# Pairing the 64-token ends of two sequences into one 128-row block, with a new order of all tasks and no filler matmuls, in a sliding-window attention and squared-ReLU kernel

## The chip, the cores and the metric

The kernel runs on one core of a Trainium2 chip, as one launch. Its time is the device time of that core in microseconds (us); the figure quoted for a kernel is the median of its runs. The engines are named as in the profile: PE is TensorE (matrix products; PEld its weight loads), DVE is VectorE, ACT is ScalarE, POOL is GpSimd, SP is SyncE. POOL here does nothing but start transfers that convert f32 to bf16 on the way in; SP starts the transposing transfers and the stores.

## The reference

The computation is attention with a causal window of 128 tokens and a linear distance bias, then a two-layer block with a squared ReLU:

```python
# q, k, v: (8 batches, 8 heads, 576 tokens, 64); w_in: (512, 2048); w_out: (2048, 512); f32
scores = scale * np.matmul(q, k.transpose(0, 1, 3, 2))
rel = pos[:, None] - pos[None, :]
mask = (rel >= 0) & (rel < 128)
scores = np.where(mask, scores + bias[None], -1000000000.0)   # bias = slope of the head * -|rel|
attn = softmax(scores)
x = np.matmul(attn, v)            # reordered to (4608 tokens, 512)
g = np.maximum(x @ w_in, 0.0) ** 2
out = g @ w_out                   # (4608, 512)
```

## The kernel before, in words

**Blocks and jobs.** A sequence of 576 tokens is cut into four blocks of 128 tokens and a last one of 64; the 40 blocks of the 8 sequences are numbered `m` = 0 to 39 in the order of the list `seq`. Blocks 0 to 3 are the first blocks of four sequences ("lone" jobs, with an additive bias). Every other block attends to itself and to the block before it. A "full" job does one 128-token block; a "half" job does the 64-token ends of two sequences together: blocks 10 and 11, 18 and 19, 28 and 29, 38 and 39. The names of tasks carry the block: `lkq10` and `lv10` load keys, queries and values (POOL; for the first blocks `lk`, `lq`, `lv`), `kqT10` transposes keys and queries by a transposing transfer (SP; for blocks 0 to 7 it is `tp`, four PE transposes each for keys and queries, with evictions `ev`), `s10.0` and `s10.1` are the scores (PE), `e10.0` to `e10.3` the exponentials (ACT), `m10.0` and `m10.1` the products with the mask (DVE), `pv10.0` and `pv10.1` the products with the values (PE), `r` and `n` the reciprocal and the normalisation (DVE), `x10` the transpose of the result into `xT` (SP; for blocks 0 to 7 `xp` on PE and an eviction).

**Half jobs before.** The two ends of a half job share the four score banks, but each is a block of its own in every other step: its own load, its own 64-row transpose `kqT`, its own 16 + 16 value products with 64 stationary columns, its own reciprocals and normalisations over 64 partitions, its own 64-row `x`. Because a 64-token block fills half of its tile, the other half of three tiles is set to zero once (`zero...` tasks).

**The two layers.** Tokens are taken in 9 groups `g` of 512. For groups 0 to 2 the first layer runs in units (`u0.1.2` is group 0, row range 1, step 2): in group 0, range 0 (the first block) steps 0 and 1 use `w_in0` and `w_in1` (two of 16 column chunks each), and steps 2, 3, 4 use `w_in2`, `w_in3`, `w_in4` (four each); in ranges 1 to 3 step 0 uses `w_in0` and `w_in1`, step 1 `w_in2`, step 2 `w_in3`, step 3 `w_in4`. From group 3 on the first layer is done by Strassen products `f3.0.1` to `f3.3.7`; the second layer is done by Strassen products `p0.1.0` to `p8.7.1` for all groups. Sums of the operands (`S`, `ut`, `us`, `ws`) are on DVE; snapshots `s1`, `s2`, `s5` and sums `c11`, `c12`, `c22` of products on ACT and DVE; squares `sq` on either; stores `st` on SP.

**Order.** Nothing is ordered by a loop. A string `ORDER` lists all 1722 tasks with the engine that does each (no letter: PE; `a` ACT, `d` DVE, `g` POOL, `s` SP) and, after it, the PSUM bank or ring buffer that it takes. Each engine carries its own tasks out strictly in the order of the string, each when its inputs, its buffers and its turn are there. `transpose_kq` makes every transposing transfer `kqT` wait for all pieces of both weight matrices. The ring of key and query tiles has four places, that of transposed ones seven, that of value tiles nine. The queue of POOL's transfers, and that of SP's, have eight semaphores each.

**Warm-up and fillers.** `warm_up` issues `N_WARM` matmuls of 512 columns on a zeroed tile before anything is there to compute. `fill` adds 128-column matmuls ahead of a task of the first 30 us where the planner expects PE to wait over 400 ns, for the part `FILL` of that wait. Both compute nothing that is used.

Of the kernel before, what the change touches and what calls it, by code (L numbers as in the profile page):

```python
# [27 lines left out]
N_WARM = 8  # L28
# [4 lines left out]
FILL = 0.4  # L33
# [15 lines left out]
NF = 8  # L49
UT = 1  # L50
# [12 lines left out]
iota:g ident:d dist1:d slope1.0:d warm0:d lk0.1:a lk0.0:s one0.1:d slope0.3:d slope1.2:a slope0.0:a one0.3:d  # L63
slope1.1:d slope0.1:a slope1.3:a ck0:a slope0.2:a warm::0 b0::1,2 lk2:g lq2:g lq0.0:s lq0.1:s lk1:g cq0:a
one0.0:d tp0.0::3 tp2.0::4 b2::5,6 tp0.1::7 tp2.1::0 ev2.0.0:d ev0.1.0:a lk3:g lq1:g tp3.0::4 ev3.0.0:a
ev2.1.0:d ev0.0.0:d one0.2:d tp1.0::7 s2 s0 e0.0:a e2.0:a e2.1:a ev1.0.0:d e0.1:a lv0:g lv2:g lq3:g lv1:g
w_in1:g w_in0:g w_in2:g lv3:g w_in3:g lk4:g lq4:g b1::0,4 tp1.1::3 pv2.0::7 ev1.1.0:d r2.0:d pv0.0::1 pv0.1::5
s1 n2.0:d r0.1:d r0.0:d n0.0:d tp3.1::3 n0.1:d xp0.0::6 pv2.1::2 x0.0:d r2.1:d ev3.1.0:d mask1.1:a e1.0:a e1.1:a
table:a pv1.0::7 pv1.1::1 b3::5,0 n2.1:d u0.0.1::4 r1.0:d r1.1:d n1.0:d n1.1:d xp2.0::6 s3 u0.0.0::3 xp1.0::2
dist0:d x2.0:a e3.0:a x1.0:a mask1.7:a reluu0.0.0:a:0 u0.2.0::7 mask0.3:a mask1.2:a mask0.1:a mask1.6:a e3.1:a  # L70
u0.1.0::1 u0.1.1::6 pv3.0::5 pv3.1::2 u0.2.1::3 u0.0.2::0 squ0.0.0:d one1.2:d reluu0.1.0:a:1 mask0.2:a
reluu0.2.0:a:2 one1.8:d r3.0:d squ0.1.0:d one1.7:d r3.1:d n3.0:d n3.1:d xp3.0::1 x3.0:d one1.5:d reluu0.2.1:a:3
one1.6:d squ0.2.1:d squ0.2.0:d reluu0.1.1:a:0 mask1.5:a mask1.4:a mask0.7:a mask0.5:a mask1.3:a mask1.0:a
reluu0.0.2:a:1 u0.1.2::7 tp4.0::5 tp4.1::2 ev4.1.0:d squ0.0.2:d u0.2.2::3 ev4.0.0:a reluu0.0.1:a:3 s4.0::6,1
s4.1::0,5 reluu0.1.2:a:2 e4.0:a lk5:g reluu0.2.2:a:1 lk6:g lq5:g lv5:g lq6:g w_in4:g tp5.0::2 u0.0.3::4
u0.3.0::7 tp5.1::6 squ0.0.1:d one1.1:d one1.0:d squ0.1.2:d ev5.0.0:d e4.1:a mask0.0:a mask0.4:a mask0.6:a m4.0:d
ev5.1.0:d squ0.1.1:d lk7:g lv4:g lv6:g lq7:g w_out3:g w_out0:g lv7:g w_out2:g w_out1:g e4.3:a reluu0.3.0:a:3
e4.2:a reluu0.0.3:a:2 squ0.3.0:d u0.3.1::2 tp6.0::3 reluu0.3.1:a:0 ev6.0.0:d tp6.1::1 s5.0::5,7 ev6.1.0:d
one1.4:d one1.3:d squ0.0.3:d s5.1::6,0 u0.3.2::4 e5.0:a s6.0::3,2 s6.1::1,5 e5.1:a e5.3:a e6.0:a e5.2:a
squ0.2.2:d m4.1:d squ0.3.1:d m5.0:d u0.1.3::7 u0.2.3::0 pv4.0::3 m5.1:d r4.0:d n4.0:d e6.2:a e6.1:a  # L80
reluu0.3.2:a:3 e6.3:a pv4.1::6 pv5.0::1 pv5.1::2 tp7.0::4 u0.0.4::3 tp7.1::5 reluu0.2.3:a:2 ev7.0.0:a
reluu0.0.4:a:1 ev7.1.0:a r5.0:d r4.1:d r5.1:d m6.0:d n5.0:d n5.1:d n4.1:d u0.3.3::0 m6.1:d xp5.0::4 xp4.0::1
pv6.0::2 reluu0.3.3:a:0 x4.0:a squ0.0.4:d x5.0:d squ0.2.3:d pv6.1::3 r6.0:d squ0.3.2:d us0.0:d us3.0:d
squ0.3.3:d S1.0.0:d s7.0::6,5 reluu0.1.3:a:1 s7.1::0,4 u1.0.3::1 e7.0:a e7.2:a e7.1:a e7.3:a u1.0.6::7 u1.0.2::6
u1.0.1::0 reluu1.0.6:a:2 squ1.0.6:a u1.0.4::5 m7.0:d n6.0:d u1.0.7::4 S2.0.0:d m7.1:d lkq9:g lkq8:g lkq10:g
lv9:g lkq11:g kqT9:s r6.1:d us1.0:d n6.1:d xp6.0::7 reluu1.0.1:a:3 reluu1.0.7:a:0 squ1.0.1:a reluu1.0.2:a:2
pv7.1::2 pv7.0::0 r7.0:d r7.1:d n7.0:d u1.0.0::3 squ0.1.3:d n7.1:d zerokqT10:d S1.0.1:d S2.0.1:d us2.0:d ws0.0:d
S3.0.0:d u1.0.5::4 xp7.0::0 p0.2.0::6 p0.1.0::2 p0.1.1 ws0.1:d kqT8:s lv8:g reluu1.0.4:a:3 x6.0:a squ1.0.2:a
x7.0:a reluu1.0.3:a:1 squ1.0.3:d u1.1.1::5 reluu1.1.1:a:2 reluu1.0.0:a:1 squ1.0.0:a squ1.0.4:d squ1.0.7:d
zerov10:d s1_0:d:0 kqT10:s ws1.0:d zerokqT11:d kqT11:s squ1.1.1:d p0.2.1 u1.1.5::7 u1.1.0::0 reluu1.1.0:a:3  # L90
reluu1.0.5:a:0 reluu1.1.5:a:1 u1.1.7::1 squ1.1.0:d ws1.2:d reluu1.1.7:a:2 u1.1.2::5 u1.1.6::3 squ1.1.7:a
reluu1.1.2:a:3 reluu1.1.6:a:2 u1.1.3::0 lkq12:g lv12:g lkq13:g lkq14:g s8.0::4,7 s8.1::1,5 ws0.2:d c11_0:d
S4.0.1:d S4.0.0:d squ1.1.5:d e8.0:a e8.1:a e8.2:a e8.3:a p0.5.0::6 u1.1.4::3 s9.0::4,7 s9.1::1,5 p0.5.1 kqT12:s
m8.0:d ws1.1:d m8.1:d reluu1.1.4:a:1 e9.0:a e9.1:a pv8.1::3 pv8.0::4 p0.6.0 p0.6.1 squ1.1.4:d S1.1.0:d
reluu1.1.3:a:1 e9.2:a s5_0:a:1 e9.3:a p0.3.0 lv10:g lv13:g lkq15:g m9.0:d r8.0:d n8.0:d squ1.0.5:d pv9.0::7
zerov11:d m9.1:d r8.1:d us0.1:d S3.0.1:d pv9.1::0 p0.3.1 lv11:g r9.1:d n8.1:d s10.0::1,4 s10.1::5,3 ws1.3:d
squ1.1.6:a s2_0:a:2 c12_0:d us3.1:d r9.0:d n9.0:d n9.1:d ws0.3:d e10.0:a e10.2:a e10.3:a m10.1:d us2.1:d e10.1:a
squ1.1.2:a x8:s p0.7.0 p1.2.0::6 p1.2.1 s12.0::1,5 s12.1::7,3 p0.7.1 lkq16:g e12.0:a e12.3:a squ1.1.3:a e12.2:a
e12.1:a x9:s m10.0:d S2.1.0:d us1.1:d pv10.0::0 pv10.1::4 pv11.0::1 c22_0:d r11.0:d p1.1.0::3 p1.1.1 p0.4.0
# [146 lines left out]
class Plan:  # L246
# [27 lines left out]
    def order(self):  # L274
# [8 lines left out]
        for item in ORDER.split():  # L283
            if item.startswith("reluc"):
                continue
# [51 lines left out]
def kernel(  # L337
# [196 lines left out]
    def zero(m, tag, slot, key, part, after):  # L534
        def run():
            if slot.turn == 0:
                nc.vector.memset(part(tile_of(slot)), 0.0)
# [917 lines left out]
```

## Time and profile before

| | |
|---|---|
| median of 3 runs | 292.15 us (291.11, 292.15, 292.66) |
| profiled execution, its own time | 291.41 us |
| its span, first to last instruction | 289.6 us |
| PE busy | 281.0 us, 3480 matmuls |
| DVE, ACT, POOL busy | 242.5, 202.3, 106.3 us |
| read from and written to memory | 36.70 MB and 9.44 MB |

The profiled execution took 1.8 us more than its span, which is what lies around the instructions; its time is 0.74 us under the median of the runs. A busy share says how much of the span an engine had an instruction under way. Matmuls overlap: one takes some 270 ns from start to end while the next starts after 109 ns, so PE's mean durations are latencies, and what a stream of them costs is read from the starts of neighbouring rows.

### The profile page before, as it was taken

How to read it: one execution, taken by the hardware profiler on the slowest of the kernel's cores; microseconds unless marked ns; L12 is line 12 of the kernel's file. 1: busy time of each engine (PE TensorE's matmuls, PEld its weight loads, DVE VectorE, ACT ScalarE, POOL GpSimd, SP SyncE). 2: the span in 40 equal slices, each digit the busy share in tenths (PEclk: the TensorE clock that was granted, in tenths of full speed). 3: DMA queues.
4: the chain of work that ended last, by engine and by line, in shares of the span. 5: the costliest groups of instructions: out<-in, count | busy, mean ns of one | idle time of the engine just before them, and what ended most of it. 6: DMA issues, size and time to landing. Idle time of an engine off the chain costs nothing.

```text
span 289.6 us, 8647 instructions
## 1 busy us (share of the span) xinstructions
PE 281.0 (97%) x3480; PEld 243.5 (84%) x3480; DVE 242.5 (84%) x570; ACT 202.3 (70%) x399; POOL 106.3 (37%) x132
## 2 busy tenths in 40 slices
PE   6999999999999999999999999999999999999994
PEld 2688999887888988888888889888898888888884
DVE  2555897799858899999899999999998988998764
ACT  4669985877388785799888978797774834845700
POOL 8967734492662940542738363060000000000000
PEclk9999999999999999999999999999999999999999
DMA  9999999999999999999999999999421122010054
GB/s 127 166 194 171 183 201 160 140 135 155 184 153 177 174 151 181 176 160 189 168 166 180 176 184 153 162 114 175 129 75 57 54 69 63 20 36 2 0 162 148
DMA packets 171495, 39.62 MB, mean 137 GB/s; under 512 B 156992, under 2 KB 171456, under 8 KB 171456
## 3 DMA queue, kind: packets, MB, share of 16 engines
q0 software_dynamic: 115184, 18.10, 88.8%
q1 hardware_dynamic: 55520, 20.39, 39.2%
q10 hardware_dynamic: 752, 0.59, 0.7%
q8 instruction: 27, 0.44, 0.6%
q14 instruction: 12, 0.10, 0.1%
HBM read 36.70 MB, written 9.44 MB: 159 GB/s over the span
## 4 chain that ended last, share of the span: by engine, by line
PE 77%; DMA 8%; POOL 7%; ACT 2%; DVE 2%; issue 1%; POOLq 0%
PE o L1246 32%; PE h L1091 25%; PE h L997 10%; PE pv L848 5%; PE s L738 5%; DMA kq<-in_q_dram 4%; DMA vt<-in_v_dram 2%; DMA kqT<-kq 2%; POOL kq L612 2%; POOL kq L618 2%; POOL vf L625 1%; POOL w_in_sb L549 1%; ACT g L956 1%; DVE P L760 1%; ACT rt L964 1%
## 5 line engine op out<-in xcount | busy, mean ns | idle before, releaser
L1246 PEld LDWEIGHTS <-g 128*128 128x128 bf16 x704 | 67.8, 98 | 8.0
L772 ACT ACTIVATE P<-s 128x512 bf16<-128x512 f32 x120 | 65.0, 620 | 6.9 <-PE s L738 6.6
L964 ACT ACTIVATE rt<-h 128x512 bf16<-128x512 f32 (+1 forms) x73 | 42.4, 602 | 22.2 <-PE h L997 11.4
L618 POOL DMA_DIRECT2D kq<-in_k_dram x32 | 27.2, 851 | 76.6 <-DMA kqT<-kq 72.6
L1246 PE MATMUL o<-w_out_sb,g 128*128 128x256 bf16 x432 | 54.0, 273 | 0.0
L1112 DVE CUSTOM_DVE_ANT_0 rt<-h,f 128x512 bf16<-128x512 f32 x72 | 48.5, 683 | 6.1 <-PE h L1091 2.8
L450 ACT ACTIVATE f<-h 128x512 f32<-128x512 f32 x63 | 36.5, 604 | 19.0 <-PE h L1091 17.5
L956 ACT ACTIVATE g<-rt 128x512 bf16<-128x512 bf16 x70 | 42.9, 636 | 6.2 <-DVE rt L1112 5.8
L997 PE MATMUL h<-xT,w_in_sb 128*128 128x128 bf16 (+1 forms) x512 | 46.6, 246 | 0.5 <-DMA w_in_sb<-in_moe_w_in_dram 0.5
L997 PEld LDWEIGHTS <-w_in_sb 128*128 128x128 bf16 x512 | 39.1, 98 | 4.7 <-DMA w_in_sb<-in_moe_w_in_dram 0.9
L1091 PE MATMUL h<-xT,w_in_sb 128*128 128x256 bf16 x288 | 41.7, 273 | 0.0
L1091 PEld LDWEIGHTS <-w_in_sb 128*128 128x128 bf16 x384 | 36.0, 98 | 5.0
L760 DVE TENSOR_TENSOR P<-P,masks 128x1024 bf16<-128x1024 bf16 x48 | 32.3, 683 | 4.1 <-ACT P L772 3.3
L1246 PE MATMUL o<-wsum,sums 128*128 128x256 bf16 x288 | 35.7, 273 | 0.0
L1246 PE MATMUL o<-wsum,g 128*128 128x256 bf16 x272 | 34.8, 273 | 0.0
L958 DVE TENSOR_TENSOR g<-rt 128x512 bf16<-128x512 bf16 (+1 forms) x75 | 29.8, 413 | 4.8 <-ACT rt L964 4.7
L625 POOL DMA_DIRECT2D vt<-in_v_dram x36 | 30.8, 871 | 4.4 <-DMA w_in_sb<-in_moe_w_in_dram 2.1
L877 DVE TENSOR_TENSOR x<-pv,rec 128x256 bf16<-128x256 f32 (+1 forms) x80 | 31.6, 414 | 0.7
L1091 PEld LDWEIGHTS <-us 128*128 128x128 bf16 x288 | 27.8, 98 | 3.5
L1246 PEld LDWEIGHTS <-sums 128*128 128x128 bf16 x288 | 27.6, 98 | 3.6
L450 ACT ACTIVATE f<-o 128x512 f32<-128x512 f32 x30 | 18.2, 608 | 14.6 <-PE o L1246 13.3
L618 POOL DMA_DIRECT2D kq<-in_q_dram x32 | 27.5, 860 | 2.0 <-PE xp L897 1.8
(79 smaller groups left out, 356.9 us busy)
## 6 DMA issues: line engine op xcount, KB each, us to landing
out_dram<-f SPq DMA_DIRECT2D x62, 128.0 KB, 2.5
kq<-in_k_dram POOLq DMA_DIRECT2D x31, 128.0 KB, 6.1
kq<-in_q_dram POOLq DMA_DIRECT2D x31, 128.0 KB, 7.0
vt<-in_v_dram POOLq DMA_DIRECT2D x28, 128.0 KB, 6.4
w_out_sb<-in_moe_w_out_dram POOLq DMA_DIRECT2D x4, 512.0 KB, 11.5
w_in_sb<-in_moe_w_in_dram POOLq DMA_DIRECT2D x3, 512.0 KB, 8.7
out_dram<-f SPq DMA_DIRECT2D x13, 64.0 KB, 2.2
vf<-in_v_dram POOLq DMA_DIRECT2D x4, 128.0 KB, 4.7
```

The lines of the kernel that those rows point to most:

```text
L450: nc.scalar.activation(o, i, AF.Copy)
L618: nc.gpsimd.dma_start(view(kq[s_kq[m].idx], i), source(src, m, split))
L625: nc.gpsimd.dma_start(tile_of(s_v[m])[0:n, :, 0:D], source(v, m))
L760: nc.vector.tensor_tensor(flat(Pt[sP.idx], w), flat(Pt[sP.idx], w), flat(masks, w), op=ALU.mult)
L772: nc.scalar.activation(flat(Pt[sP.idx], slice(2 * i, 2 * i + 2)), sS[i].tile.rearrange("p (j t) -> p j t", j=2)[:, :, lo:hi], AF.Exp, bias ...
L877: nc.vector.tensor_tensor(o, heads(sv)[0:n, :, 0:D], sr.tile[0:n, :].unsqueeze(2).to_broadcast([n, 4, D]), op=ALU.mult)
L956: nc.scalar.activation(o, i, AF.Square, bias=0.0, scale=1.0)
L964: nc.scalar.activation(rts[srt.idx][:, 0:n], slot.tile[:, 0:n], AF.Relu, bias=0.0, scale=1.0)
L997: nc.tensor.matmul(slot.tile[:, f * w:(f + 1) * w], w_in_sb[:, cc, fc * 128:(fc + 1) * 128], xT[:, cc, lo % (XR * 128):lo % (XR * 128) + w ...
L1091: nc.tensor.matmul(slot.tile[:, j * 256:j * 256 + 256], a, b_, start=fresh and j == 0 and c == 0, stop=c == 1, skip_group_check=True)
L1112: nc.vector._custom_dve(TENSOR_ADD_SAT, out=rts[srt.idx], in0=slot.tile, in1=other(), s0=FMAX, s1=0.0)
L1246: nc.tensor.matmul(slot.tile[:, z * 256:z * 256 + 256], stationary(c), moving(c), start=fresh and z == 0 and c == 0, stop=c == F - 1, skip ...
```

## The change

1. **Ends paired.** The ends of two sequences become one block of 128 rows under the number of the first (10, 18, 28, 38): they are loaded into the two halves of one tile (six transfers as before, of 64 rows each), transposed by one `kqT`, normalised by two `r` and two `n`, and transposed by one `x`. The tasks of blocks 11, 19, 29 and 39 and the `zero` tasks are gone. A new mask `pmask` (`pm0`, `pm1`, `pm2`) is built once in the place of two tiles of the first blocks, after the scores that read these tiles.
2. **Value products of a pair.** Eight products with 128 stationary columns against the pair's own values, then sixteen with 64 stationary columns, alternately for the first and the second sequence, whose results go to partitions 0 to 63 and 64 to 127.
3. **A new `ORDER`** of 1677 tasks, on each engine and in all banks; 43 tasks move from DVE to ACT, 38 from ACT to DVE, two stores from SP to ACT.
4. **`FILL` 0.4 to 0.0, `N_WARM` 8 to 12.**
5. **Dependencies.** Products `f.1` and `f.2` wait for the first half of their group's tokens only; tiles of values, of the first blocks' keys and of `ut` are given free by each reader; the second part of `S1` and `S2` comes after the first.

```diff
-N_WARM = 8
+N_WARM = 12
-FILL = 0.4
+FILL = 0.0
...
+    pmask = kqf[:, 0:2].rearrange("p l c t -> p (l c t)").rearrange("p (h r t) -> p h r t", h=H, r=2)
...
+    def load_pair(m, key):
...
+                for j in range(2):
+                    o = kq[s_kq[m].idx][64 * j:64 * j + 64, i * d_model:(i + 1) * d_model]
+                    nc.gpsimd.dma_start(o.rearrange("s (h d) -> s h d", h=H), source(src, m + j))
...
-            pieces = [(part * 128 + i * 64, 64, part, (before[m], m)[part], m)
-                      for part in range(2) for i, m in enumerate(ms)]
+            pieces = [(i * 64, 64, before[m], ms[0], i * 64) for i, m in enumerate(ms)] + [(128, 128, ms[0], ms[0], 0)]
...
+        def pv_pair():
...
+            for h in range(H):
+                sv, hi = svs[h // 4], h % 4
+                nc.tensor.matmul(sv.tile[:, hi * (D + 1):(hi + 1) * (D + 1)], Pt[sP.idx][:, place(h), 1],
+                                 tile_of(s_v[m])[:, h, 0:D + 1], start=hi == 0, stop=False, skip_group_check=True)
+            for h in range(H):
+                sv, hi = svs[h // 4], h % 4
+                for i2, mk in enumerate(mb):
+                    nc.tensor.matmul(sv.tile[64 * i2:64 * i2 + 64, hi * (D + 1):(hi + 1) * (D + 1)],
+                                     Pt[sP.idx][:, place(h), 0, 64 * i2:64 * i2 + 64],
+                                     tile_of(s_v[mk])[:, h, 0:D + 1], start=False, stop=True, skip_group_check=True)
...
-        rel = [s_t] if u == 3 and p in (4, 5, 6) else []
-        tm = plan.add({"PE": 4 * mm(256)}, key, emit, deps + st["x"],
+        rel = [s_t] if p in (4, 5, 6) else []
+        tm = plan.add({"PE": 4 * mm(256)}, key, emit, deps + st["xe" if p < 3 else "x"],
```

The head of the order, PE's tasks alone, before and after:

```
before: warm b0 tp0.0 tp2.0 b2 tp0.1 tp2.1 tp3.0 tp1.0 s2 s0 b1 tp1.1 pv2.0 pv0.0 pv0.1 s1 tp3.1 xp0.0 pv2.1 pv1.0
        pv1.1 b3 u0.0.1 xp2.0 s3 u0.0.0 xp1.0 u0.2.0 u0.1.0 u0.1.1 pv3.0 pv3.1 u0.2.1 u0.0.2 xp3.0 u0.1.2 tp4.0 tp4.1 ...
after:  warm tp0.0 tp3.0 tp0.1 b3 b0 tp1.0 s0 tp3.1 s3 tp1.1 tp2.0 b1 tp2.1 pv0.1 pv3.0 s1 pv3.1 b2 pv1.0 pv0.0 xp3.0
        pv1.1 tp4.0 s2 xp0.0 xp1.0 u0.0.2 pv2.0 u0.1.1 tp4.1 pv2.1 u0.3.1 u0.0.1 s4.0 s4.1 xp2.0 u0.1.0 u0.2.1 u0.3.0
        u0.2.0 u0.3.2 u0.0.0 tp5.0 tp7.0 tp5.1 ...
```

And of POOL:

```
before: iota lk2 lq2 lk1 lk3 lq1 lv0 lv2 lq3 lv1 w_in1 w_in0 w_in2 lv3 w_in3 lk4 lq4 lk5 lk6 lq5 lv5 lq6 w_in4 lk7 lv4
        lv6 lq7 w_out3 w_out0 lv7 w_out2 w_out1 lkq9 ...
after:  iota lk2 lk3 lk1 lq3 lq2 lq1 lv0 lv3 lv1 lk4 w_in2 lv2 lq4 w_in1 w_in0 lk5 w_in3 lk7 lq5 lq7 lv4 w_in4 lv5 lv7
        lk6 lq6 w_out0 w_out1 lv6 lkq10 lkq8 w_out3 lkq9 w_out2 lv9 ...
```

More of the change, by code (lines that the diff above doesn't have):

```diff
@@ L62 @@
 ORDER = """
[L63 to L67, printed above, removed]
@@ L83 @@
[L83 to L87, printed above, removed]
@@ L530 @@
                                  name=f"one1.{i}", later=20000.0)
[L534 to L537, printed above, removed]
-        return plan.add({"DVE": 220.0}, key, run, [], [slot], name=f"zero{tag}{m}", later=25000.0, after=after)
     t_win = [None] * FCB
@@ L702, in job @@
         nb = len(ms)
-        n = 64 if kind == "half" else 128
-        for m in ms:
+        for m in ms[:1] if kind == "half" else ms:
             transpose_kq(m, due)
@@ L1055, in prepare_up @@
         xs = [x for m in blocks(g * 512, g * 512 + 512) for x in t_x[m]]
+        xe = [x for m in blocks(g * 512, g * 512 + 256) for x in t_x[m]]
         ts = []
```

260 lines of the change are left out of this document (72 added, 188 removed).

## The prediction

> **What bounds the kernel now.** I read the page first (busy times, slices, chain), then PE's waits, then PE's timeline.
>
> ```profile
> span 289.6 us, 8647 instructions
> PE 281.0 (97%) x3480; PEld 243.5 (84%) x3480; DVE 242.5 (84%) x570; ACT 202.3 (70%) x399; POOL 106.3 (37%) x132
> ...
> PE   6999999999999999999999999999999999999994
> ...
> PEclk9999999999999999999999999999999999999999
> DMA  9999999999999999999999999999421122010054
> ...
> PE 77%; DMA 8%; POOL 7%; ACT 2%; DVE 2%; issue 1%; POOLq 0%
> ```
>
> PE never leaves nine tenths after the first slice: the time is PE's head, the sum of PE's work, the few holes, and the tail. The transfers are as full as PE until 215 us. PE's waits, in total (engine, line, releaser: us, times, longest):
>
> ```profile
> PE wm L649 <- DVE sums L468: 2.5, 1, 2.5
> PE pv L848 <- DMA vt<-in_v_dram: 0.5, 1, 0.5
> PE pv L848 <- ACT P L813: 0.5, 2, 0.3
> PE h L997 <- DMA w_in_sb<-in_moe_w_in_dram: 0.5, 1, 0.5
> PE tp L681 <- DMA kq<-in_q_dram: 0.5, 1, 0.5
> ```
>
> Only 4.5 us are waits. Four stand before 25 us; the other, 0.5 us at 70 us, is for the values of block 11. So there is little to win in the middle. From PE's timeline (start, us, what, count) and the chain of waits, the rows for the prices:
>
> ```profile
> 2.50 3.59 PE L649 MATMUL wm<-sums 128*128 128x512 bf16 x8 [2.50 <-DVE sums L468]
> 5.88 1.06 PE L796 MATMUL s<-sums,ident 128*128 128x512 bf16 x2
> ...
> 19.51 1.07 PE L997 MATMUL h<-xT,w_in_sb 128*128 128x128 bf16 x16 [0.47 <-DMA w_in_sb<-in_moe_w_in_dram]
> ...
> 24.61 0.40 PE L681 MATMUL tp<-ident,kq 128*128 128x128 bf16 x4 [0.45 <-DMA kq<-in_q_dram]
> ...
> 51.06 5.40 PE L997 MATMUL h<-xT,w_in_sb 128*128 128x256 bf16 x48
> 56.39 0.23 PE L738 MATMUL s<-kqT,kqT 64*128 64x128 bf16 x2
> ...
> 56.94 1.05 PE L1246 MATMUL o<-wsum,sums 128*128 128x256 bf16 x8
> ...
> 112.65 1.04 PE L1246 MATMUL o<-wsum,sums 128*128 128x256 bf16 x8
> 113.62 1.20 PE L848 MATMUL pv<-vt,P 128*64 128x65 bf16 x32
> 114.75 0.61 PE L1091 MATMUL h<-xT,w_in_sb 128*128 128x256 bf16 x4
> ```
>
> ```profile
> 13.98 10.58 DMA kq<-in_q_dram
> 26.79 1.79 PE h L997 x32
> ...
> 47.51 6.37 DMA kqT<-kq
> ...
> 64.15 6.68 DMA vt<-in_v_dram
> ...
> 271.74 12.23 PE o L1246 x112
> 283.97 1.78 PE o L1348 x24
> ```
>
> Prices: 12.23 / 112 = 109 ns for 256 columns, 1.79 / 32 = 56 ns for 128. Scores: the 48 matmuls before them end their issue at 51.06 + 48 x 0.109 = 56.30, the scores start at 56.39 and give way at 56.94; their eight pairs of row halves stream 8 x 0.056 = 0.45. So a run of scores costs 0.19 us beyond its work, 0.09 to go in and 0.10 to go out. A run of 64-column value products costs the same: 113.62 - (112.65 + 8 x 0.109) = 0.10 to go in, then 1.13 for 32, of which 32 x 0.0315 = 1.01 stream and 0.1 goes out.
>
> **The head.** I measure PE by its lag: the start of a task less the useful PE work ahead of it in the order, at these prices (value products 30 ns, a pair of 512-column bias matmuls 0.43 us). Ahead of the first scores of block 8 stand 256 unit matmuls of 128 columns (14.3 us), 15 units of group 1 and 4 products of 8 x 0.109 (16.6), 24 groups of four transposes (5.4), biases and lone scores (3.3), four score jobs (2.5) and the value products (2.8): 44.9 us. They start at 56.39, lag 11.5. At `tp4.1`, the row at 24.61, 13.3 us stand ahead: lag 11.3. There the lag was made, by queries 4, which landed at 13.98 + 10.58 = 24.56; afterwards PE loses almost nothing. So the new lag decides, and the new lag is set by when weights land.
>
> ```profile
> w_in_sb<-in_moe_w_in_dram POOLq DMA_DIRECT2D x3, 512.0 KB, 8.7
> ...
> kq<-in_q_dram POOLq DMA_DIRECT2D x31, 128.0 KB, 7.0
> ```
>
> ```profile
> 5.00:10.00 5.00, 4.86 (x39) 2.91 (x37) 1.39 (x4) 1.77 (x3) 5.00 (x6) 1.00 2.33 157
> 34.00:37.00 3.00, 3.00 (x72) 3.00 (x70) 2.58 (x11) 2.98 (x7) 2.21 (x3) 1.00 1.25 206
> 30.00:40.00 10.00, 10.00 (x207) 9.34 (x205) 9.18 (x29) 9.95 (x21) 5.33 (x7) 1.00 1.69 188
> ```
>
> The last column is GB/s: 128 KB of keys at 157 take 0.84 us, 512 KB of weights at 206 take 2.5. Queries 4 were the 12th block after 12 chunks of weights (1.25 us for two). In the new order of POOL `w_in2` has 10 blocks ahead and is chunks 1 to 4: 24.56 - 2 x 0.84 - 8 x 0.63 = 17.8. `w_in0` has 12 blocks and completes 8 chunks: 24.56 - 2.5 = 22.0. `w_in3` has 13 blocks and 12 chunks: 25.4. The PE work ahead of their first users is 6.75 us (`u0.0.2`), 11.2 (`u0.1.0`) and 14.75 (`u0.3.2`): lags 11.1, 10.8, 10.6. The new head is bound by `w_in2`, lag 11.1: it gains 0.4 us. Other bound: should the early `w_in2` come sooner than the later anchor says, `w_in3`, one block behind that anchor, still holds the lag at 10.6, a gain of 0.9. On the other side ACT could be the limit:
>
> ```profile
> L495 ACT ACTIVATE masks<-sums 128x128 bf16<-128x128 f32 x16 | 3.9, 311 | 0.0
> ```
>
> 18 evictions at 9.95 / 21 = 0.47 and 13 masks at 3.9 / 16 = 0.24 make 11.6 us between the start of `u0.0.2` and the end of `u0.2.2`, whose PE work is 10.9: 0.7 more lag, a loss of 0.3. I take the gain of 0.4, because most of those masks can wait for a later eviction.
>
> **Warm-up and fillers: zero.** The fillers are these:
>
> ```profile
> L429 PE MATMUL pv<-sums 128*128 128x128 bf16 x9 | 0.8, 219 | 0.0
> L429 PE MATMUL xp<-sums 128*128 128x128 bf16 x7 | 0.6, 219 | 0.0
> ```
>
> 16 x 0.056 = 0.9 us, all ahead of value products and transposes that then waited for data before 15 us. `warm` stands behind two small memsets in the new order of DVE instead of mask preparation, so it can start near 1.4 instead of 2.50; 12 x 0.42 ends near 6.5 (before: 5.88). PE then has 6.75 us of work for the 11.4 us until `w_in2`, so 4.6 us cover it. Without that cover four more warm matmuls cost 4 x 0.42 = 1.7.
>
> **The pairs.** Before, the ends' value products are 32 matmuls per job in seven runs of the order (blocks 10/11 two, 18/19 one, 28/29 one, 38/39 three). After: 8 of 128 columns and 16 of 64 per job, four runs. Removed 4 x 8 x 0.030 = 0.96 and 3 x 0.19 = 0.57. The scores of a pair stay (16 row-half pairs of 64 against 8 of 64 and 4 of 128), but the new order has 35 runs of scores for 33: +0.38. Sum: -1.15 us of PE work, all on the path. Unknown is a 64-column matmul whose neighbour uses the other column half: as dear as now (0.0315), as cheap as the row halves, which go two in 56 ns, so half the price (another 4 x 16 x 0.016 = 1.0 off), or a change of mode each time (below). I take the first, the nearest row. By the Trainium skill, TensorEngine Tiling (Array Packing), Key Properties, a change of the mode drains the engine but different tiles load and multiply in parallel; the 0.10 at each end agrees, and with the parallel halves the sum would be 1.0 us better. No run so far shows column halves in turn.
>
> DVE loses half of these (off the path, DVE being 84% busy):
>
> ```profile
> L864 DVE RECIPROCAL rec<-pv 64x4 f32<-64x4 f32 x16 | 2.5, 166 | 1.3 <-PE pv L848 1.2
> L877 DVE TENSOR_TENSOR x<-pv,rec 64x256 bf16<-64x256 f32 x16 | 6.4, 408 | 0.2
> ```
>
> 4.4 us less; the mask copies `pm0`, `pm1` go to ACT (about 1 us each, 70% busy) long before block 10's mask. POOL issues as many transfers; SP eight transposes fewer:
>
> ```profile
> L666 SPq DMA_TRANSPOSE kqT<-kq x32: 1193/1414/4038, 47.5 to 196.5; - x32
> ...
> DMA to landing us min/median/max: 2.6/6.1/10.9
> ```
>
> That frees 8 x 1.4 = 11 us of SP, which nobody waits for.
>
> **The holes.** The wait of 0.5 at 70 us goes: values 10 and 11 are one load, ahead of `lv13`, and `pv10` has 63.1 us of work ahead, 74.2 with the lag, against 64.15 + 6.68 = 70.8 for the old landing of the last end. What is late next: the shortest distance between a product and the one that must wait for its snapshot is 0.87 us of PE work in the new order (five places) for 0.91 in the old, where PE waited nowhere; 0.04 short five times, +0.2. The looser dependencies (part 5) remove waits that the trace doesn't have: zero.
>
> **Sum.** -0.4 - 1.15 - 0.5 + 0.2 = -1.9 us: 287.7 span, 289.5 for the profiled execution. That lies 0.7 under the median, so for the median 292.15 - 1.9 = 290.2. For scale, about 0.5%, 1.5 us, is what a measurement here can tell from no change: this lies just beyond. With the bounds above (-0.9 - 2.15 - 0.5 = -3.55; +0.3 - 1.15 - 0.5 + 0.5 = -0.85) the likeliest case runs from 288.6 to 291.3.
>
> **Rivals.**
>
> *The order gives back what the pairs win (no difference).* ACT is late in the new head (+0.3 instead of -0.4), and five snapshots and one load stall 0.2 more each (+1.2): 290.2 + 0.7 + 1.2 = 292.1. For it: the whole order is new, and ACT has 11.6 us of work for 10.9 of PE's. Against: distances that matter have grown (median from scores to value products 5.7 us to 10.0 of PE work). Chance 0.20.
>
> *Transposes come late (slower).* All `kqT` wait for all weights. Before, `kqT9` went at 47.51, when queries 9, two blocks behind the last weight, had landed: the weight landed at 45.8. `w_out2`, now the last weight, stands behind `lkq10` (four half blocks), `lkq8` and `lkq9` (four blocks) besides: 45.8 + 4 x 0.42 + 4 x 0.84 = 50.9. `kqT8` is third on SP, issued at 50.9 + 2 x 1.4 = 53.7; the scores of block 8 have 48.5 us of work ahead, 59.6 with the lag, and block 8's exponentials, masks and value products queue behind them. A latency up to 5.9 costs nothing, the median 6.1 costs 0.2; from 5.9 + 1.9 + 1.5 = 9.3 on it makes the kernel slower by over 1.5 us, and the longest, 10.9, costs 5.0: 295.2. For it: the 6.37 of the first transpose lay on the chain. Against: that one was the first of its burst, and the third is issued 2.8 us later, into fewer loads. Chance 0.12.
>
> *Column halves change mode (slower).* 16 matmuls x 4 jobs x 0.10 = 6.4: 296.6. Only a change of tile size shows 0.10; a change of row half shows none. Chance 0.06.
>
> *The clock falls without fillers.* PE has nothing to do for 4.6 us in all before 17.8, spread by loads that arrive one by one; the first matmuls show a slow clock, (5.88 - 2.50) / 8 = 0.42 us for 512 columns where 256 later take 0.109. A fall would cost half of a stretch like that of these rows, (5.88 - 2.50) / 2 = 1.7 us: 291.9, no measurable difference. By the Trainium skill, TensorE: Matmul & The Clock Gate, Part 1 (The HAM clock gate), an idle window of about 3.4 us halves the clock; no gap in this trace is long enough to show it, the longest wait after the start being 0.5. Between arrivals some work always falls due, so I expect under 3 us in one piece. Chance 0.06.
>
> **How the numbers follow.** Likeliest case 0.56, of which 0.51 over 1.5 us faster (up to 290.7) and 0.05 between that and 291.3; return 0.20 and clock 0.06 end level; late transposes 0.12 and mode changes 0.06 end slower. So faster 0.51, same 0.05 + 0.20 + 0.06 = 0.31, slower 0.18. The range takes in the likeliest case, a little lower for prices rounded up, and the two that end level, to 293.3; it leaves out what is slower.
>
> **What would show it.** Right: 3480 - 16 - 64 + 4 = 3404 matmuls and the first unit at 17.5 to 18.2; block 8's scores at 59 to 60 without a wait; a pair's value products in 0.9 us; PE's waits after 20 us under 1 us; last matmul near 283.7. Wrong: PE waiting on kqT near 60 us, matmuls of 0.1 us in the pairs, 107 ns units near 18 us, or PE idle before ACT's results between 18 and 31 us.

## The result: 304.3 us, 3.6% slower than before

The changed kernel took 304.29 us (median of four runs; 301.16 to 306.15), the kernel before, run beside it, 292.40. The ratio of their runs is 1.036, with a 95% interval of 1.024 to 1.048. The prediction, 290.2 with a range up to 293.3, was wrong in sign. Ratios, here and below, leave out runs over 1.5% above the fastest of the same kernel, which the medians still contain; where a median and a ratio seem to disagree (e12, e17), that is why.

The profiled execution took 304.97 us. Its page:

```profile
span 302.8 us, 8461 instructions
PE 282.4 (93%) x3403; PEld 242.2 (80%) x3404; DVE 241.8 (80%) x557; ACT 203.9 (67%) x397; POOL 106.3 (35%) x132
...
PE   7889999899589999899899976999999999999995
...
PEclk9999999999899999999999998999999999999999
...
PE 54%; DMA 30%; POOL 8%; SPq 3%; issue 3%; ACT 1%; DVE 0%; POOLq 0%; ACTq 0%; DVEq 0%
```

PE, under nine tenths before in the first and the last slice alone, now falls below it in seven slices between 50 and 200 us; the granted clock falls in two of them; and transfers hold 30% of the chain that ended last, where they held 8%. Who waited (in total, times, longest):

```profile
POOL kq L480 <- DMA kqT<-kq: 59.4, 11, 11.7
...
ACT f L294 <- DMA out_dram<-f: 8.3, 4, 2.8
...
PE pv L715 <- DMA vt<-in_v_dram: 3.8, 1, 3.8
...
DVE f L292 <- DMA out_dram<-f: 2.7, 1, 2.7
PE s L609 <- DMA kqT<-kq: 2.5, 2, 1.2
PE o L1135 <- DVE f L292: 2.4, 1, 2.4
...
PE h L980 <- ACT f L294: 2.3, 3, 1.3
...
PE h L885 <- DMA xT<-x: 1.0, 1, 1.0
```

POOL's long wait for transposes is not new. Before, it was longer:

```profile
POOL kq L618 <- DMA kqT<-kq: 72.6, 15, 11.0
```

Two families of new waits are to be seen. In the first, PE waits for what transfers bring: values of pair 10, transposed keys, transposed rows. In the second, PE waits for a snapshot (`f`) that ACT or DVE could not write, because the buffer was still being stored. Before, ACT and DVE never waited for a store to write a snapshot; here they do for 11 us, of which 1.2 stand at 292 us, in the tail. The chain of waits shows one of each (start, us, what):

```profile
45.15 8.42 DMA kq<-in_q_dram
53.57 6.92 DMA kqT<-kq
...
66.21 9.60 DMA kq<-in_q_dram
...
79.68 8.41 DMA xT<-x
...
88.23 1.91 PE h L885 x16
...
180.34 5.44 DMA out_dram<-f
185.86 0.70 DVE f L292
186.60 1.87 PE o L1135 x8
```

From 45 to 88 us no step of the chain is computation: a load lands at 53.6, its transpose at 60.5; that frees the place for the next loads, of which one lands at 75.8; SP issues the transpose of that one and only then, in its strict order, the store and the rows `xT` that PE takes at 88.2. At 186 us a store lands, the snapshot takes its buffer, and PE goes on.

The clock, by stretches (length, PE busy and matmuls, ..., granted clock in the third column from the end):

```profile
79.00:80.00 1.00, 0.81 (x25) 0.75 (x26) 0.12 (x1) 0.00 (x0) 0.66 (x2) 1.00 1.59 158
80.00:81.00 1.00, 1.00 (x9) 0.86 (x9) 1.00 (x5) 0.00 (x0) 0.22 (x1) 0.83 1.92 167
83.00:84.00 1.00, 1.00 (x24) 0.91 (x18) 0.00 (x0) 0.96 (x2) 1.00 (x2) 0.50 2.22 153
84.00:85.00 1.00, 1.00 (x13) 0.80 (x9) 0.00 (x0) 0.78 (x2) 0.34 (x1) 0.96 1.88 208
```

The wait of 3.8 us ends at 79.2; from 80.7 to 84.1 the clock is half. It is half again from 186.5 to 189.9, around the end of the wait of 2.4. The mean granted clock of the execution is 0.988, so 302.8 x 0.012 = 3.6 us of matmul time are lost, 3.4 of them in these two falls of 3.41 us each (the rest lies at the very end).

**Where the time lies.** For each pair of neighbouring matmuls I take the time between their starts less the price of the first (0.215 us for 512 columns, 0.109 for 256, 0.056 for 128, 0.029 for 65, half of that for scores in row halves) and add up, from the first matmul on, which starts at 2.5 us before and at 1.3 after. By this sum PE's work is 266.1 us before and 264.9 after; what is lost beyond it (us, profiled executions):

| lost in | before | after | e6 | e14 | e16 | e5 | e15 |
|---|---|---|---|---|---|---|---|
| 0 to 50 us | 7.7 | 8.5 | 8.6 | 8.7 | 8.9 | 7.0 | 8.5 |
| 50 to 100 | 3.4 | 9.6 | 10.3 | 6.9 | 3.5 | 3.5 | 2.3 |
| 100 to 200 | 4.3 | 12.9 | 6.1 | 5.0 | 4.7 | 4.5 | 5.0 |
| later | 1.6 | 1.6 | 1.3 | 1.1 | 1.0 | 0.7 | 0.8 |

The work fell by 1.2 us, close to the 1.15 forecast; the loss behind 50 us rose by 14.8. The rest of this document is about that rise.

### The profile page after: what moved, and what is told of

The parts are those of the page before. It is cut to its first block, busy times and chain, and to the rows that moved or that the text cites. A ratio compares the mean times of both kernels' runs of the same rounds, so it can differ in the third digit from the quotient of the medians.

```text
span 302.8 us, 8461 instructions
## 1 busy us (share of the span) xinstructions
PE 282.4 (93%) x3403; PEld 242.2 (80%) x3404; DVE 241.8 (80%) x557; ACT 203.9 (67%) x397; POOL 106.3 (35%) x132
## 4 chain that ended last, share of the span: by engine, by line
PE 54%; DMA 30%; POOL 8%; SPq 3%; issue 3%; ACT 1%; DVE 0%; POOLq 0%; ACTq 0%; DVEq 0%
PE o L1135 24%; PE h L980 19%; DMA out_dram<-f 8%; DMA kq<-in_q_dram 8%; PE h L885 5%; DMA kqT<-kq 4%; DMA w_out_sb<-in_moe_w_out_dram 4%; DMA w_in_sb<-in_moe_w_in_dram 3%; PE s L609 3%; DMA xT<-x 3%; POOL kq L474 3%; PE pv L738 2%; SPq L540 2%; POOL kq L480 2%; ACT f L294 1%
## 5 line engine op out<-in xcount | busy, mean ns | idle before, releaser
L641 ACT ACTIVATE P<-s 128x512 bf16<-128x512 f32 x120 | 65.9, 610 | 12.9 <-PE s L609 12.8
L1001 DVE CUSTOM_DVE_ANT_0 rt<-h,f 128x512 bf16<-128x512 f32 x72 | 48.2, 685 | 10.6 <-PE h L980 6.5
L294 ACT ACTIVATE f<-h 128x512 f32<-128x512 f32 x61 | 35.5, 601 | 23.4 <-PE h L980 10.7
L480 POOL DMA_DIRECT2D kq<-in_k_dram x24 | 21.5, 895 | 60.5 <-DMA kqT<-kq 59.4
L980 PE MATMUL h<-xT,w_in_sb 128*128 128x256 bf16 x288 | 40.1, 273 | 0.5 <-ACT f L294 0.4
L1135 PE MATMUL o<-wsum,sums 128*128 128x256 bf16 x288 | 37.7, 281 | 2.9 <-DVE f L292 2.4
L1135 PEld LDWEIGHTS <-sums 128*128 128x128 bf16 x288 | 28.4, 100 | 7.3 <-issue 3.5
L765 DVE TENSOR_TENSOR x<-pv,rec 128x256 bf16<-128x256 f32 x72 | 29.1, 419 | 1.0
L485 POOL DMA_DIRECT2D vt<-in_v_dram x28 | 25.4, 923 | 4.7 <-DMA vt<-in_v_dram 2.9
L980 PE MATMUL h<-ut,us 128*128 128x256 bf16 x192 | 26.1, 273 | 0.6 <-ACT f L294 0.6
```

Source lines behind the costliest of these rows:

```text
L294: nc.scalar.activation(o, i, AF.Copy)
L480: nc.gpsimd.dma_start(view(kq[s_kq[m].idx], i), source(src, m, split))
L641: nc.scalar.activation(flat(Pt[sP.idx], slice(2 * i, 2 * i + 2)), sS[i].tile.rearrange("p (j t) -> p j t", j=2)[:, :, lo:hi], AF.Exp, bias ...
L765: nc.vector.tensor_tensor(o, heads(sv)[0:n, :, 0:D], sr.tile[0:n, :].unsqueeze(2).to_broadcast([n, 4, D]), op=ALU.mult)
L980: nc.tensor.matmul(slot.tile[:, j * 256:j * 256 + 256], a, b_, start=fresh and j == 0 and c == 0, stop=c == 1, skip_group_check=True)
L1001: nc.vector._custom_dve(TENSOR_ADD_SAT, out=rts[srt.idx], in0=slot.tile, in1=other(), s0=FMAX, s1=0.0)
```

## The experiments

### Which part of the change: pairs, fillers or order

**e5, the pairs on the old order.** The changed kernel's code, with the order of before adapted where it must be. The rule that the second part of `S1` and `S2` comes after the first is left out, since the old order has `S1.2.1` ahead of `S1.2.0`; on DVE the new order keeps that sequence by itself.

```diff
-... lkq9:g lkq8:g lkq10:g lv9:g lkq11:g lv8:g ...   pv10.0::0 pv10.1::4 pv11.0::1 ... pv11.1::7 ...
+... lkq9:g lkq8:g lkq10:g lv9:g lv8:g ...           pv10::1,7 r10.0:d n10.0:d ...
```

> Edit: the changed kernel's code with the order of before, its tasks adapted only where they must be: the tasks of blocks 11, 19, 29, 39 and the zero tasks are taken out, a pair's value products stand where the last of the four stood, its reciprocal, normalisation and transpose behind them, its loads where those of the first block stood, the pair's mask behind the exponentials and masks of block 7. Theory (the pairs are worth what the sum said, the new order costs): -1.15 us of PE work, a further -1.0 because the column halves run in parallel, the wait of 0.5 for block 11 gone: 289.5 to 291 us. Rival (the pairs cost: four loads of keys and queries of 64 rows and two of values come late and products wait for them): a wait near 70 us as in the changed kernel, 295 to 300.

Measured: 290.57 us, ratio 0.9947 (0.9917 to 0.9977). The pairs gain on the old order, and it holds them without new waits for transfers behind 50 us; the four 64-row loads cost nothing. There is a new wait of 0.9 us for a bank, at 72.8 us. The looser dependencies of part 5 are in this kernel too and were not tried alone. From PE's timeline, pair 10:

```profile
71.70 0.41 PE L850 MATMUL pv<-vt,P 128*128 128x65 bf16 x8
72.04 0.44 PE L855 MATMUL pv<-vt,P 128*64 128x65 bf16 x16
72.42 0.20 PE L873 MATMUL pv<-vf,P 128*128 128x65 bf16 x1
```

The sixteen products with 64 columns take 72.42 - 72.04 = 0.38 us with the way out. By the starts of the single rows they go in eight pairs, the two of a pair 3 to 4 ns apart and a pair every 29 to 36 ns (the second 49 ns behind the first), so some 16 to 17 ns each, where such a product took 31.5 before: the column halves run in parallel.

**e3 and e4, the fillers alone.**

```diff
 e3, on the changed kernel:          e4, on the kernel before:
-N_WARM = 12    -FILL = 0.0          -N_WARM = 8    -FILL = 0.4
+N_WARM = 8     +FILL = 0.4          +N_WARM = 12   +FILL = 0.0
```

> Edit: the changed kernel with N_WARM 8 and FILL 0.4 as before. My theory: the fillers act in the first 30 us only and the clock falls near 80 and 185 us, so nothing changes: within 1 us of the changed kernel (303 to 305). Rival (the clock falls for want of fillers): 2 to 4 us faster, about 301.

> Edit: the kernel before with N_WARM 12 and FILL 0.0, its order kept. My theory: no measurable difference, 292 to 293 us (warm starts at 2.5 and would end 1.7 us later, before the first data that PE waits for has landed). Rival: the clock falls without fillers or the warm-up ends too late: 294 us or more.

Measured: e3 305.53 us (ratio 1.0395, 1.030 to 1.049), no better than the changed kernel; e4 292.66, ratio 1.0023 (0.9975 to 1.007). Neither shows the fillers to be worth anything. Since the pairs on the old order are no slower either, what costs 12 us and more is the new order.

### The late stores

**e6, ten buffers for snapshots and stores instead of eight.**

```diff
-    VS = 96
+    VS = 72
-NF = 8
+NF = 10
...
+                    if s.tag == "f":
+                        s.idx = ...   # the buffer that has been free longest
```

> Edit: the changed kernel with ten buffers f for snapshots and stores instead of eight (each taken by the one free longest; value tiles are padded to 72 columns a head instead of 96 to make room). Theory (late stores hold the buffers: snapshots on ACT waited 8.3 us and on DVE 2.7 us for stores to land, and PE waits for the snapshots): the holes at 121, 147, 178 and 184 us (1.5 + 1.3 + 1.4 + 2.55) and the slow clock behind the last go, the first 90 us stay: 295 to 298 us. Rival (the same transfers that make stores late make the transposed rows late, so PE then waits for those): 301 to 304.

Measured: 298.16 us, ratio 1.0228 (1.0202 to 1.0254). Its waits:

```profile
PE s L747 <- DMA kqT<-kq: 3.6, 3, 2.4
...
PE h L1023 <- DMA xT<-x: 1.6, 1, 1.6
...
ACT f L432 <- DMA out_dram<-f: 1.2, 1, 1.2
```

ACT waits 1.2 us for stores instead of 8.3, and that in the tail, DVE not at all, and PE loses 6.1 us instead of 12.9 between 100 and 200 us. So snapshots held up by stores are shown to be a part of the loss: 6.1 us by the medians, 1.3%, some 4 us, by the ratios. In the changed kernel the stores themselves take no longer than before: of those issued ahead of 200 us, half land within 5.1 us of their issue, and within 5.7 in the kernel before. So what differs is when they are issued, or when the buffers are taken: ahead of ACT's wait at 122 us SP issues none from 99.3 to 114.6 us, where transposes stand, and then eight within 6.1 us. Whether SP's strict order alone does this was not separated. Up to 100 us nothing is better.

### The first hundred microseconds: one move at a time

**e1, the transposes of 10 and 8 first; e2, the values of 10 early.**

```diff
 e1:                                     e2:
-kqT9:s kqT10:s kqT8:s lv9:g            -lkq15:g lkq13:g lkq16:g lv15:g lkq14:g lv12:g lv10:g
+kqT10:s kqT8:s kqT9:s lv9:g            +lv10:g lkq15:g lkq13:g lkq16:g lv15:g lkq14:g lv12:g
```

> Edit: the changed kernel with one move in SP's order: kqT9 goes behind kqT10 and kqT8 (blocks 10 and 8 were loaded at 41.9 and 43.6 us, block 9 at 47.8; SP takes its tasks strictly in order). Theory A (one late root: the transposes of 10 and 8 stand behind one that waits for a later load, so the ring of key and query tiles comes free 8 us late and all that follows is late): kqT10 issues near 42 instead of 49.5, the load of block 15 near 51 instead of 58.7, the values of block 10 land near 72 instead of 79.1; PE's waits at 59 us (1.4), 75 us (3.8), 87 us (1.2) and the slow clock behind the second go; later waits shrink too: 292 to 296 us. Theory B (the new order asks everywhere for transfers earlier than the transfer engines can bring them): kqT10 is issued early but the later loads gain under 2 us, the waits move on: 301 to 304 us.

> Edit: the changed kernel with one move in POOL's order: the values of block 10 ahead of the keys and queries of block 15 (before them stood 15, 13, 16, values 15, 14, values 12). Theory A (late root): the values still wait for nothing of the ring (values have their own ring), so they go near 47 us instead of 68; the wait of 3.8 at 75 us and the slow clock behind it (about 1.9) go, the others stay: 298 to 300 us. Theory B: what is put ahead costs the others as much: the wait moves to values 15 or 12 or to transposes: 302 to 305 us.

Measured: e1 303.03 us (ratio 1.0315, 1.0225 to 1.0405), e2 304.43 (1.0378, 1.029 to 1.047). Theory A, one late root, falls. In e1 the transposes went at 42.1 and 43.7, but the six loads asked for between 41.5 and 45.7 us landed 4.6 to 6.1 us later than in the changed kernel, `w_out2` at 56.7 instead of 51.1, and PE waited for that:

```profile
49.75 2.78 PE L1020 MATMUL h<-xT,w_in_sb 128*128 128x256 bf16 x24
56.79 1.46 PE L1270 MATMUL o<-w_out_sb,g 128*128 128x256 bf16 x6 [4.26 <-DMA w_out_sb<-in_moe_w_out_dram]
```

In e2 the values landed at 57.5 and the wait for them was gone; PE waited for the transpose of block 14 instead:

```profile
84.44 0.29 PE L744 MATMUL s<-kqT,kqT 64*128 64x128 bf16 x2 [3.55 <-DMA kqT<-kq]
```

**e11, the hole filled**, to hold the clock up.

```diff
+            if m == 10:
+                for _ in range(16):
+                    nc.tensor.matmul(svs[0].tile[:, 0:512], ident, w_in_sb[:, 0, 0:512], start=True, stop=True)
```

> Edit: the changed kernel with 16 idle matmuls of 512 columns (3.4 us) ahead of the value products of block 10, in the hole of 3.8 us at 75 us; their result is overwritten. Theory (a hole of this length drops the clock to half for some 3.5 us behind it, price 1.7 to 1.9): 1.5 to 2 us faster than the changed kernel, 302 to 303, and the clock 1.00 from 79 to 84 us. Rival (the slow clock has another cause, or what it loses is waited for anyway further on): 304 to 305.

Measured: 304.32 us, ratio 1.0411 (1.036 to 1.046): nothing gained. By stretches, the granted clock in the third column from the end:

```profile
79.00:84.00 5.00, 4.92 (x72) 3.96 (x71) 3.81 (x10) 3.25 (x7) 1.75 (x2) 1.00 2.49 126
84.00:87.00 3.00, 0.75 (x16) 0.52 (x15) 1.95 (x6) 0.78 (x2) 1.53 (x2) 1.00 1.88 171
...
88.00:89.00 1.00, 1.00 (x7) 0.69 (x6) 0.00 (x0) 0.40 (x1) 0.10 (x1) 0.50 1.79 252
```

The clock stayed full where it was expected to. But PE then met the next two transfers earlier, waited 1.06 us up to 85.0 and 1.36 up to 87.1, and the clock fell at 87.6. The rival is right in this run: what the clock gives back is waited for.

**e9, six places for key and query tiles instead of four; e10, five places and ten buffers.**

```diff
-SIZE = {"kq": 4, ...
+SIZE = {"kq": 6, ...      # e10: 5, and NF = 10
```

> Edit: the changed kernel with six places for key and query tiles instead of four (value tiles padded to 72 columns a head instead of 96 to make room; eight buffers f as in the changed kernel). Theory R (the ring: POOL stood still from 47 to 58.7 us because the fifth load waits for the transpose of block 10 to land): the loads of blocks 15 and 13 go near 47, the values of block 10 land near 70 instead of 79, the holes at 75 and 87 and the slow clock between them go: 296 to 299 us. Theory T (a transposing transfer takes as much of the transfer engines as three loads, and they have no idle time there): the loads that go early delay the transposes of 8 to 10, PE waits 3 us more at 59, and the sum stays: 302 to 305.

> Edit: five places for key and query tiles and ten buffers f (value tiles padded to 68 columns). Theory R: to the 298.2 of ten buffers f alone it adds most of what six places bring: 293 to 296. Theory T: 297 to 299.

Measured: e9 310.88 us, ratio 1.0622 (1.056 to 1.068), 6.6 slower than the changed kernel; e10 298.82 (1.0233, 1.0175 to 1.029), as with ten buffers alone. Waits of e9:

```profile
ACT f L429 <- DMA out_dram<-f: 9.5, 3, 5.7
PE s L744 <- DMA kqT<-kq: 7.6, 2, 4.6
...
PE o L1270 <- ACT f L429: 4.4, 1, 4.4
```

POOL's stop of 11.7 us is not the cause. When POOL may run ahead, its loads delay the transposes that PE needs next (4.6 us at 59 us instead of 1.2), and stores with them. Theory T had the place and the size of the wait on PE, and underrated what the stores would add.

### Order against need, and sheer cost

**e7 and e8, cheaper loads, after and before.**

```diff
+        if m >= N_PE and t is not v:
+            r = b * H * S + kb * 128 * H
+            return t.rearrange("b h s d -> (b h s) d")[r:r + blk[kb] * H].rearrange("(s h) d -> s h d", h=H)
         return s.rearrange("h s d -> s h d")
```

> Edit: the changed kernel, but keys and queries of the later single blocks are read from rows that lie together in memory (as many bytes, 2 KB at a stretch instead of 256 bytes), so that these transfers are cheaper; values computed from them are others. Pairs and values are loaded as before. Theory (the new order asks for transfers earlier than they come): PE's waits behind 50 us mostly go, 291 to 295 us. Rival (the holes come from the order of SP and of the buffers, whatever a transfer takes): 300 to 304.

> Edit: the same cheaper reads of keys and queries in the kernel before. My theory: it waits for transfers for 0.5 us behind 25 us only, so it gains at most 1 us: 291 to 292.5. Rival (transfers bound the kernel before as well): 288 or less.

Measured: e7 299.84 us, ratio 1.0205 (1.016 to 1.025); e8 291.51, ratio 0.9995 (0.9973 to 1.0017). On one point the first expectation is wrong: pairs go through the same function, so their keys and queries are read in the cheap way as well, and only the values as before. The packet counts further below agree: 24 blocks of 2 x 1024 packets and 8 ends of 2 x 512, each now an eighth, make 50176 fewer. Cheaper transfers help the new order, though the intervals of the two ratios still touch and e7's median lies between its two forecasts; they do nothing for the old one. They do not cure the new one: 11.3 us are still lost between 100 and 200 us, and ACT and DVE still wait for stores there, 3.1, 1.5 and 2.5 us.

**e13 and e14, the transfers of 35 to 60 us in the order of PE's need; e14 with ten buffers too.**

```diff
-lkq10:g lkq8:g w_out3:g lkq9:g w_out2:g     kqT9:s kqT10:s kqT8:s
+lkq8:g w_out3:g w_out2:g lkq9:g lkq10:g     kqT8:s kqT9:s kqT10:s
```

> Edit: the changed kernel with the transfers of 35 to 60 us asked for in the order in which PE needs them: POOL takes block 8, w_out3, w_out2, block 9, block 10 (changed kernel: 10, 8, w_out3, 9, w_out2), SP transposes 8, 9, 10, 12 (changed kernel: 9, 10, 8, 12). Theory O (order against need): w_out2 lands before the product at 52 us, the transpose of block 8 well before 59, the ring is free for the next load near 51 instead of 58.7; the waits at 59 and 75 us and the slow clock behind go: 297 to 300 us. Theory T (transfers are short by the same amount whatever comes first): waits of the same sum elsewhere, 303 to 305.

> Edit: both, the order by need and ten buffers f. Theory O: both gains add, 291 to 294 us, near the prediction's 290.2. Theory T: 297 to 299 as with ten buffers alone.

**e16, cheap loads and ten buffers; e17, e14 with two more moves by need.**

```diff
 e17:
-lkq16:g lv15:g lkq14:g       kqT16:s kqT14:s st1.2.0:s x8:s
+lkq14:g lkq16:g lv15:g       kqT14:s st1.2.0:s x8:s kqT16:s
```

> Edit: the changed kernel with cheaper reads of keys and queries (as in e7_cheap_loads_after; values computed from them are others) and ten buffers f. If late stores and late loads are the two parts and nothing else is lost: 299.8 - 6 = 293 to 294 us. If they are one shortage seen twice: 296 to 298.

> Edit: e14_by_need_ten_f, and two more moves: POOL loads block 14 ahead of block 16, SP transposes block 16 behind the rows of block 8 (order there: 14, store, rows 8, 16; scores of 14 run at 82 us, of 16 at 91). Theory O: the holes at 79.7 and 82.7 us (2.4 + 1.6) and the slow clock behind them (1.3 to 1.9) go: 290.5 to 292 us. Theory T: the wait moves to scores 16 or a later block, 294 to 296.

Measured: e13 301.85 us (ratio 1.0333, 1.0275 to 1.039), e14 295.97 (1.0134, 1.008 to 1.0185), e16 292.93 (1.0023, 0.9989 to 1.0057), e17 293.64 (0.9973, 0.9925 to 1.0022). The page of e16, queue by queue (packets, MB, share of 16 engines), whose row in the changed kernel is the second fence:

```profile
PEclk9999999999999999999999999999999999999999
...
q0 software_dynamic: 65008, 18.10, 69.5%
```

```profile
q0 software_dynamic: 115184, 18.10, 86.1%
```

The same megabytes, in 56% of the packets, keep the engines busy for 0.695 x 288.1 = 200 us instead of 261. In this execution, the fastest of e16's ten (290.35 us), little is left of the two families: PE waits once behind 50 us, 1.4 us for a transpose at 80, no snapshot waits for a store ahead of the tail, and the clock doesn't fall. By the ratio the new order is then level with the kernel before, as the first of the two sums had it.

The order by need takes the first family away without cheaper transfers. In e13 PE goes from 49.8 to 59.5 us without a wait, and from e6 to e14 to e17 the loss between 50 and 100 us is 10.3, 6.9 and 2.9. e13 alone is not told from the changed kernel by its ratio; e14 against e6 is (1.0134, at most 1.0185, for 1.0228, at least 1.0202). So theory O holds in its direction: what the new order asks for first is not what PE needs first. It is a part of the truth only. The medians of e13, e14 and e17 each lie between what theory O and theory T forecast. e17 comes level by its ratio, but its median is 1.8 us above that of the kernel before (291.88), and six of its twelve runs lie over 294 us, where two of 23 do before. Its profiled execution (294.63 us) still waits at 107, 166 and 177 us and loses 9.6 us between 100 and 200. Where these later waits come from was not tried.

### A version faster than both

**e12, e15 and e18: the pairs on the old order** with other banks for two value products, then with ten buffers, then with the fillers of before.

```diff
 e12:                          e15: VS = 72, NF = 10 as in e6
-pv10::1,7    -pv18::7,6       e18: N_WARM = 8, FILL = 0.4
+pv10::4,7    +pv18::7,5
```

> Edit: the pairs in the order of before, as in e5_pairs_old_order, but the value products of pair 10 go to banks 4 and 7 (not 1 and 7) and those of pair 18 to 7 and 5 (not 7 and 6), since PE waited 0.9 and 0.3 us for banks that were still being read. Expected: the two waits go, 1.0 to 1.3 us faster than that, 289.3 to 289.6 us, the fastest so far. Rival (what follows then waits for the normalisation on DVE instead): 290.5.

> Edit: pairs in the order of before with the other banks (e12_pairs_other_banks) and ten buffers f. That kernel's profiled execution lost 3.4 us at 191 us to one snapshot that waited 3.7 us for a store. Expected: that scatter goes, runs between 288 and 291, median near 289.5. Rival (in such runs it is the transfers that are late, the buffer only shows it first): the same scatter, median 290.5 to 292.

> Edit: e15_pairs_ten_f with N_WARM 8 and FILL 0.4 as before. My theory: no measurable difference, 289.5 to 290.5 us. Rival (fillers keep the clock up in the first 20 us): 289 or less.

Measured: e12 292.35 us, ratio 0.9945 (0.9902 to 0.9988); e15 290.12, ratio 0.9937 (0.9907 to 0.9967); e18 289.98, ratio 0.9938 (0.9909 to 0.9967). e12's gain of 1 us did not show; its twelve runs scatter from 288.5 to 295.8, and its profiled one lost 3.4 us at 191 us to a snapshot that waited for a store. With ten buffers all twelve runs of e15 lie between 288.35 and 292.23, but those of e18, with ten buffers too, reach 295.28, so it isn't shown that the buffers cure the scatter. The fillers again make no difference. The pairs, with what came with them, are a gain of 0.5 to 0.6% over the kernel before (e5, e12, e15, e18 alike), if the order around them is kept.

## Why the prediction was wrong, point by point

**The head: a little better, and not for the reason given.** `w_in2` landed at 16.3 us for the 17.8 forecast, and the first unit started at 16.4 (forecast 17.5 to 18.2). PE was ready for the scores of block 8 at 59.1 us, with 48.5 us of work ahead: lag 10.6 for 11.1 forecast and 11.5 before. That is the number of the other bound, but by luck: `w_in3`, which was to set it, landed at 24.9 and PE didn't wait for it. What set the lag are short waits, the last of them 0.44 us at 19.0, for queries 4.

**Warm-up and fillers: zero, right** in the time (e3, e4, e18).

**The pairs: right in sign and mechanism, a little small.** The row of half-array products was the wrong neighbour; the row halves were the right one. By the Trainium skill, TensorEngine Tiling (Array Packing), Key Properties, different tiles load and multiply in parallel; two products in some 32 ns, for one in 31.5 before, agree. So the sum that holds is 2.15 + 0.5, and the new waits for banks, 0.9 and 0.3 us, leave 1.45 of it. The kernel with the pairs on the old order gained 1.5 us by the ratio (291.52 x 0.0053), though its interval, 0.7 to 2.4, would allow the smaller sum too, and e12, which removes the two waits, showed no gain.

**The holes: the step that failed.** It said -0.5 + 0.2; the loss behind 50 us rose by 14.8, clock included. Three errors stand in it.

First, the values of pair 10 were given the landing of the old end, 70.8 us, though their place in POOL's queue had moved behind the keys and queries of four blocks. They landed at 79.1, for a product ready at 75.2:

```profile
79.19 0.40 PE L715 MATMUL pv<-vt,P 128*128 128x65 bf16 x8 [3.82 <-DMA vt<-in_v_dram]
```

"POOL issues as many transfers" was true and no answer: each waits for those ahead of it. In e2, ahead of these, they landed at 57.5.

Second, "what is late next" was read from distances of PE work between a product and its snapshot (0.87 for 0.91 us). A snapshot also needs a buffer, and that is free when a store has landed. The page before showed no such wait, so the buffers were not costed; e6 puts 4 to 6 of the lost microseconds there.

Third, SP was said to have 11 us to spare that nobody waits for. What counted was not its load but its order: the transposes of blocks 10 and 8, loaded at 41.9 and 43.6 us, stood behind that of block 9, loaded at 47.8. Moving these two alone won nothing that was clear of noise (e1); moving the loads with them did, with ten buffers (e14).

**The rival of late transposes came true in the number and not in the reason.** Issue of `kqT8`: 53.57, forecast 53.7. PE waited 1.25 us for it, forecast 0.2 at the median latency. But no transpose waited for the weights: `kqT9` was issued at 47.88, 0.08 us after its own queries landed, and `w_out2` landed at 51.1. So on the chip that dependency held nothing up; the strict order of SP did it, with the transpose of block 10, whose issue took 4.0 us, between the two. That the forecast time came out is luck.

**The rival of the clock had the price and not the place.** 1.7 us a fall was forecast; two falls cost 3.4 of matmul time. They came with holes in the middle, which the forecast did not see, and not in the head. Two other kernels without fillers did show a fall of 3.4 us in the head, at 15.2 us (e4) and 14.9 (e15); none of the profiled executions with fillers did, and the times don't tell them apart. By the Trainium skill, TensorE: Matmul & The Clock Gate, Part 1 (The HAM clock gate), an idle window of about 3.4 us halves the clock; here a stop of 2.4 us was enough (up to 186.6 us), and one of 3.2 us in e12 was not; the last section says why.

**The chances.** Slower had 0.18, from two mechanisms that were priced one at a time. The waits of the first family have one thing in common, a list that asks for transfers in an order that PE doesn't need them in. That could be read from `ORDER`: among blocks 8, 9 and 10 block 10 is loaded first, and its scores are needed last.

## What to carry to other kernels

An order with fewer stalls on paper can be worse on the chip when it moves transfers: for each one that is moved, work out its landing from what stands ahead of it in its new queue, never from where its predecessor landed in the old one, and compare it with the PE work ahead of its first user. For every buffer that a store empties, count the landing of the store as part of the step that takes it. When a dozen transfers share full engines, asking for one sooner only passes the wait on; sort them by need, or make them cheaper.

## What the runs showed of the hardware

Transposing transfers are dear beside loads: two of them, each of 128 rows of keys and queries, started early in e1, and the six loads asked for beside them landed 4.6 to 6.1 us later than in the changed kernel. By the 5.6 us of `w_out2` that is some 2.8 us each, where the prediction's 128 KB load took 0.84. This is an estimate from landings of one execution each.

Reading keys and queries 2 KB at a stretch instead of 256 bytes lowered the busy time of the load queue by 23% (261 to 200 us) for the same megabytes, and did not make a kernel faster that wasn't waiting for them (e8).

The clock does not follow the length of a stop, but PE's idle share in windows of 3.41 us. In every profiled execution with more than one fall their starts lie whole multiples of 3.413 us apart (changed kernel: 80.66, 186.48 and, at the end, 302.53 us, 31 and 34 of them), and a fall inside the span lasts one window, in e2, e6 and e13 two. Counted window by window in the 20 traces, from 30 us on and where the clock was full: behind each window in which PE was idle for 56% or more, the next is at half clock (29 cases, the lowest share 0.559 in e6), and behind none with 55% or less (the highest 0.551, in the changed kernel from 73.8 to 77.3 us). So the stop of 2.4 us, 2.26 of it in one window (66%), was enough, and so were e11's two short stops, which share one window and fill 63% of it. A stop of 3.2 us in e12 was not, since it fell half into one window and half into the next, 47% each. The ends of matmuls are modelled in these traces, so the shares are a little uncertain, and the two falls near 15 us (e4 and e15, 43%) stand outside the rule. Of e12 these are PE's row and the stretch (clock 1.00):

```profile
194.56 0.60 PE L1115 MATMUL h<-ut,us 128*128 128x256 bf16 x4 [3.20 <-DVE f L427]
```

```profile
194.00:196.00 2.00, 1.44 (x14) 1.11 (x15) 2.00 (x5) 0.81 (x2) 0.23 (x1) 1.00 1.30 255
196.00:198.00 2.00, 2.00 (x31) 1.75 (x31) 2.00 (x6) 2.00 (x5) 2.00 (x4) 1.00 0.65 78
```
